# Two pairs of small matmuls put side by side in a fused transformer block, and two column loads put later

## The chip, the cores and the metric

The kernel runs on one core of one Trainium2 chip. A core has TensorE (PE, matrix products, accumulating in eight PSUM banks), VectorE (DVE), ScalarE (ACT), GpSimd (POOL) and SyncE (SP), which in this kernel does nothing but issue DMAs; sixteen DMA engines carry them out. The metric is the device time of one execution in microseconds. The times of the kernel before are 783.44, 783.46 and 783.54 us, median 783.46.

## The reference

One transformer block on 2048 tokens of width 1024: a linear attention with 32 heads, then a gated feed-forward network of width 3584, both modulated by a vector `c`.

```python
mod = (_silu(c) @ w_mod).reshape(c.shape[0], 6, 1, -1)
sa, ca, ga, sb, cb, gb = (mod[:, 0], ..., mod[:, 5])
h = _layernorm(x) * (1 + ca) + sa
x = x + ga * attention(h, wqkv, wo)
h = _layernorm(x) * (1 + cb) + sb
x = x + gb * (gelu(h @ w_gate) * (h @ w_up) @ w_down)
```

In the attention, `phi(t) = where(t > 0, t + 1, exp(t)) + 1e-06` is taken of the queries and keys, and

```python
kv  = einsum('bhsd,bhse->bhde', pk, v)
z   = einsum('bhsd->bhd', pk)
num = einsum('bhqd,bhde->bhqe', pq, kv)
den = einsum('bhqd,bhd->bhq', pq, z) + 1e-06
o   = num / den
```

Each of the six vectors of `mod` has 1024 values. `sa` and `ca` are the first shift and scale, `ga` the first gate, `sb` and `cb` the second shift and scale, `gb` the last gate.

## The kernel before

**Stages.** The first normalization, keys and queries fill the first 127 us. Then, up to about 192 us, comes the stage that the change edits: 24 tiles of `m_tile` (line 895), each 16 matmuls that sum over all tokens the product of keys and inputs; from these come, for each group of four heads, `kv_prod` (line 913, eight products with the value weights, masked by VectorE into `kvt`, line 917) and `w2_pair` (line 1196, `kvt` times the output weights, copied by ScalarE into `w`, line 1198). From about 192 us on `wo_mm` (line 1266) multiplies the scaled queries with `w`, 16 chunks of 128 tokens, each followed by VectorE's addition to `x` (x1, line 1274), the statistics and normalized rows of the second normalization on ScalarE and GpSimd, and a DMA transpose into `h2a` or `h2b` (line 703). At 242 us the first products of the feed-forward network begin (line 1440). They read transposed rows that have been modulated by the second scale and shift (`mod2`, line 724, on VectorE; `mod2_act`, line 753, on ScalarE), sums of them (`s_sum`, tile `ss`, line 1395) and sums of the gate and up weights (`t_sum`, tile `tp`, line 1415). The rest of the span is this network.

**The vectors of mod.** `sa` and `ca` are made at the start. `ga`, `sb`, `cb` and `gb` are made by VectorE in pieces of 512 columns: eight accumulations per piece (`macc`, lines 816 and 819, and 796 and 798 for `gb`), which leave on each partition a part of the sum, then a split into a high half (ScalarE, lines 825 and 803) and a low half (VectorE, lines 829 and 804; tiles `hl` and `hlg`), both bf16. `mod_rows` (line 840) sums these over the partitions with matmuls by a 128x32 matrix of ones: four pieces at a time, each to its own 32 partitions of one PSUM bank, first the four high, then the four low ones. `mod_store` copies the bank with ScalarE (line 847) and stores four partitions to DRAM (line 849). From there `ga` and `gb` are loaded as rows spread over the partitions (`row_load`, line 855), `sb` and `cb` as columns of 128 partitions x 8 (line 1213): elements of 4 bytes. `cb1` (line 1749) adds 1 to the scale on VectorE.

**den.** `den` (line 1223) multiplies a masked `z` (tile `z32`) of 128x32 with the queries, 64 matmuls for all tokens in two calls: `den0` for the first two token groups of 512, `den1` for the other two. A call has eight rounds of four matmuls to 32 partitions each. VectorE adds 1e-6 (line 1228) and takes the reciprocal (line 1229) into one tile `rdc`; SyncE stores it (line 1231), and `rb_load` (line 1243) loads it back, spread over 32 partitions at a time, four loads of 256 KB per half of a token group. `pq_scale` (line 1256) multiplies the queries by it.

**What sets the order.** TensorE's and SyncE's instructions run in the order in which the program writes them. `HOOK` (line 1284) says what is written behind which of the 24 tiles: `modp` is the rows of `sb` and `cb`, `gbr` those of `gb`. For VectorE, ScalarE and GpSimd a planner (`reorder`) sorts the instructions of the stage up to the chunks of `wo_mm` by due times, which it works back from who reads a result; what is written after that keeps the written order (`SLOT`, beside the chunks). Every DMA of SyncE is in one queue, on one of eight lanes in turn, and is issued only when the DMA eight places before it has landed. A bank, a tile or a lane that is used again waits for its last user by semaphores, which the program derives from what each instruction reads and writes.

Of the kernel before, what the change touches and what calls it, by code (L numbers as in the profile page):

```python
# [38 lines left out]
OFF_TMP = OFF_GUH + 4096  # L39
# [11 lines left out]
OFF_ROW = OFF_CONST + 4096  # L51
# [279 lines left out]
def bass_adaLN_cond__linear_attn_block__geglu_ffn__prompt_kernel(  # L331
# [18 lines left out]
    with ExitStack() as es:  # L350
# [6 lines left out]
        def at(name, shape, dty, off):  # L357
            return nc.alloc_sbuf_tensor_at(name, shape, dty, offset=ABASE + off, align_bytes=4)
# [46 lines left out]
        MROW = [at(f"mrow{i}", [P, 512], f32, OFF_ROW + i * 2048) for i in range(2)]  # L405
        MROW0 = at("mrowa", [P, 256], f32, XHO[2])
        WMG = [at(f"wmg{i}", [P, 4, 512], bf16, HBO[3] + i * 4096) for i in range(2)]
        MRG = at("mrg", [P, 256], f32, OFF_TMP + 4096)
        HLG = at("hlg", [P, 2, 2, 512], bf16, OFF_TMP)
# [35 lines left out]
        def r_sm(name):  # L445
            return [(SMO[name], SMO[name] + SMSZ[name], name)]

        def r_smc(name, c_, w):
            return [(SMO[name] + c_ * w, SMO[name] + (c_ + 1) * w, name)]

        def r_x(c_, c0=0, c1=D):
            return [(OFF_XALL + (c_ * HP + c0) * 2, OFF_XALL + (c_ * HP + c1) * 2, "xall")]
# [24 lines left out]
        def r_wv(g):  # L477
            return [(OFF_WK + g * 2048, OFF_WK + (g + 1) * 2048, "wv")]
# [4 lines left out]
        def r_pq(sg, k0=0, k1=NG, s0=0, s1=SGW):  # L483
            return r_t8(PQO[sg], f"pq{sg}", k0, k1, s0, s1)
# [19 lines left out]
        def r_w(off, name, dc, c0=0, c1=D):  # L504
            return [(off + (dc * D + c0) * 2, off + (dc * D + c1) * 2, name)]
# [25 lines left out]
        def r_rb(i, h, g0=0, g1=NG):  # L531
            return [(OFF_RB[i] + (h * NG + g0) * 1024, OFF_RB[i] + (h * NG + g1) * 1024, f"rb{i}")]

        def r_2k(off, name):
            return [(off, off + 2048, name)]
# [7 lines left out]
        def pr(b):  # L543
            return [(b * 2048, (b + 1) * 2048)]

        def PS(b, c0=0, c1=512):
            return ps_all[:, b * 512 + c0: b * 512 + c1]
# [18 lines left out]
        def pset_writer(b, o):  # L566
            for t_ in pr(b):
                sch.ps.set_writer(t_[0], t_[1], o)
# [94 lines left out]
        def ln_nmean(c_):  # L663
            gop(lambda e: e.tensor_scalar(MVA[:, c_, 0:1], STA[:, c_, 0:1], -1.0 / D, None, op0=ALU.mult), rd=r_smc("st", c_, 48), wr=r_smc("mv", c_, 8), note=f"nmean {c_}")
# [119 lines left out]
        def gb_load(j, q):  # L784
            sch.dma(Q, lambda e: e.dma_start(WMG[q][:], wm_v[:, 4 * q:4 * q + 4, (10 + j) * 512:(11 + j) * 512]), wr=r_wmg(q), note=f"wmg{j}.{q}")
# [3 lines left out]
        def r_hlg(j, h):  # L789
            return [(OFF_TMP + (2 * j + h) * 1024, OFF_TMP + (2 * j + h + 1) * 1024, "hlg")]  # L790
# [15 lines left out]
        o_gb = [None]  # L806

        def gb_rows():
            mod_rows(((0, 2, 5, lambda j, h: (HLG[:, j, h, :], r_hlg(j, h))),))
            o_gb[0] = mod_store(2, 5, MRG, [(OFF_TMP + 4096, OFF_TMP + 5120, "mrg")], 2)  # L810

        def mod_acc(k, dc):
            i, a = k % 2, k % 2
# [18 lines left out]
        def mod_rows(parts):  # L832
            for k0, n, bank, src in parts:
                o = None
                w = n * P
                for h in range(2):
                    for j in range(4):
                        ap, rng = src(k0 + j * n // 4, h)
                        ap = ap[:, j * w % 512:j * w % 512 + w]
                        o = sch.op(T, lambda e, h=h, j=j, ap=ap, bank=bank, w=w: e.matmul(  # L840
                            ps_all[32 * j:32 * (j + 1), bank * 512:bank * 512 + w], ONES[:, :], ap, start=(h == 0), stop=(h == 1)),
                            rd=rng + r_sm("ones"), pwr=(pr(bank) if h == j == 0 else ()), note=f"modr{k0}.{h}.{j}")
                pset_writer(bank, o)

        def mod_store(n, bank, dst, rng, row):
            w = n * P
            sch.op(A, lambda e: e.activation(dst[:, 0:w], ps_all[:, bank * 512:bank * 512 + w], ACTF.Copy),
                   prd=pr(bank), wr=rng, note=f"mrow{row}")
            return sch.dma(Q, lambda e: e.dma_start(scr_row[row, 0:n, :].rearrange("a (h b) -> (a h) b", b=w), dst[0:128:32, 0:w]), rd=rng, note=f"mrow{row}.st")
# [309 lines left out]
        for g in range(NG):  # L1159
            task(nk + g // 2, lambda g=g: sch.dma(Q, lambda e: e.dma_start(WV[:, g, :, :], wqkv_v[:, :, 2 * D + g * P:2 * D + (g + 1) * P]),  # L1160
                                                  wr=r_wv(g), note=f"wv{g}"))
# [45 lines left out]

        def mod_pass():
            assert mdone[0] >= 48 and not late
            mod_rows(((2, 4, 5, hl_src),))  # L1210
            o_r = mod_store(4, 5, MROW[1], r_2k(OFF_ROW + 2048, "mrow1"), 1)
            for dst, nt, a0 in ((SBT, "sbT", 0), (CBT, "cbT", 2)):
                sch.dma(Q, lambda e, dst=dst, a0=a0: e.dma_start(dst[:, :], scr_row[1, a0:a0 + 2, :].rearrange("a (b p) -> p (a b)", p=P)),
                        wr=r_sm(nt), deps=[o_r], note=nt)

        HW = SGW // 2

# [20 lines left out]
        def rb_load(sg, hs=(0, 1)):  # L1238
            i = sg % 2
            for h in hs:  # L1240
                made = []
                for k in range(HPG):
                    made.append(sch.dma(Q, lambda e, h=h, k=k: e.dma_start(
                        RB[i][32 * k:32 * (k + 1), h, :, :].rearrange("p a b -> p (a b)"),
                        scr_rd[sg, h, k:k + 1, :, :].rearrange("k g t -> k (g t)").to_broadcast([32, NG * HW])),
                        wr=r_rb(i, h) if k == 0 else (), deps=made[0].deps if k else [o_rd[sg // 2]], note=f"rb{sg}.{h}.{k}"))
                rb_ops[sg, h] = made
# [13 lines left out]
        def wo_mm(c_, b0, gs):  # L1261
            sg, ci = divmod(c_, CPG)
            last = [None, None]
            for g in gs:
                for half in range(2):
                    last[half] = sch.op(T, lambda e, g=g, half=half: e.matmul(  # L1266
                        PS(b0 + half), PQ[sg][:, g, ci * P:(ci + 1) * P], W2[:, g, half * 512:(half + 1) * 512],
                        start=(g == 0), stop=(g == NG - 1)),
                        rd=r_pq(sg, g, g + 1, ci * P, (ci + 1) * P) + r_w(OFF_WK, "w2", g, half * 512, (half + 1) * 512),
                        pwr=(pr(b0 + half) if g == 0 else ()), note=f"wo c{c_} g{g} h{half}")  # L1270
            if gs[-1] == NG - 1:
                for half in range(2):
                    pset_writer(b0 + half, last[half])
                x1_ops[c_] = sch.op(V, lambda e: e.scalar_tensor_tensor(XALL[:, c_, :], ps_all[:, b0 * 512:(b0 + 2) * 512], 1.0, XALL[:, c_, :],
                                                           op0=ALU.mult, op1=ALU.add, accum_out=STA[:, c_, 0:1]),
                       prd=pr(b0) + pr(b0 + 1), rd=r_x(c_), wr=r_x(c_) + r_smc("st", c_, 48),
                       deps=[s_ops[0, 0, 1]] if c_ == 13 else [], note=f"x1 c{c_}")
                if c_ < 2 * CPG:
                    ln_nmean(c_)
# [1 line left out]
        wo_load(0)  # L1281
        wo_load(1)
        tiles = [(g, k) for g in range(4) for k in range(3)] + [(g, 0) for g in range(4, NG)] + [(g, k) for g in range(4, NG) for k in (1, 2)]
        HOOK = {0: "ga", 6: "kv0", 8: "w0", 9: "kv1", 11: "w1", 12: "kv2", 14: "w2 modp", 15: "kv3 z32", 16: "den0", 17: "w3 rb0.0 rb0.1", 18: "",
                19: "kv4", 20: "w4 den1 ps0.0", 21: "gbr", 22: "ps0.1", 23: "rb2.0"}
        st = {}

        def hook_run(f):
            if f[:2] == "kv":
                kv_prod(int(f[2:]), 4)  # L1290
            elif f == "ga":
                ga_pass()
            elif f == "gbr":
                assert mdone[0] == 64
                gb_rows()
            elif f == "modp":
                mod_pass()
            elif f == "z32":
                z32()
            elif f[:3] == "den":  # L1300
                st[int(f[3:])] = den(int(f[3:]), 5)
                st[int(f[3:])]()
            elif f[:2] == "ps":
                pq_scale(int(f[2]), int(f[4]), GH[0] + GH[1])
            elif f[:2] == "rb":
                rb_load(int(f[2]), (int(f[4]),))
            elif f[0] == "w":
                w2_pair(int(f[1:]))

        for n, (g, k) in enumerate(tiles):  # L1310
# [13 lines left out]
            if n == 11:  # L1324
                gb_load(1, 0)
                gb_load(1, 1)
            for f in HOOK.get(n, "").split():
                hook_run(f)
# [8 lines left out]
        wo_mm(1, 2, E6[5:])  # L1337
        rb_load(1)
        rb_load(2, (1,))
        wo_mm(2, 4, E6[:4])  # L1340
        w2_pair(7)
        wo_mm(2, 4, E6[4:])
# [624 lines left out]
```

## Time and profile before

| | |
|---|---|
| median of 3 runs | 783.46 us |
| the profiled execution | 783.52 us |
| its span | 781.7 us |
| TensorE busy | 774.5 us, granted clock 1.0 |
| VectorE, ScalarE busy | 641.9 us, 376.3 us |
| `sbT` and `cbT`, issue to landing | 3.2 us, 3.1 us |
| rb loads, issue to landing, median | 6.9 us |

In a timeline a row is one instruction or a run of equal ones: its start in us from the span's start, its length, engine, line, operation, tile written and tiles read, shape, and in brackets how long the engine sat idle before it and what ended that. For matmuls `128*32` is the part of the array used. SPq is SyncE's DMA queue; its length is the time of issuing, not of the transfer. A stretch lists each engine's busy time and number of instructions, then the granted clock, the mean busy share of the sixteen DMA engines and what they moved.

### The profile page before, as it was taken

To read this page: it belongs to the slowest core of one execution; us is meant where nothing else is said; L and a number is where in the kernel's file an instruction comes from. 1 tells how busy PE (TensorE), PEld (TensorE's weight loads), DVE (VectorE), ACT (ScalarE), POOL (GpSimd) and SP (SyncE) were. 2 spreads that over 40 slices of the span, in tenths; PEclk is the share of its full clock that TensorE was granted. 3 is DMA by queue.
4 is the path that set the end of the run, shared out by engine and by line. 5 is a ranking of instruction groups with operands and counts; after the bars stand their busy time and mean duration, and the time that the engine had idled before them with its cause. 6 is when DMAs were issued, how large, how long until landed. Compare 5 with 4: busy or idle time off the path is not lost.

```text
span 781.7 us, 10762 instructions
## 1 busy us (share of the span) xinstructions
PE 774.5 (99%) x3867; PEld 497.4 (64%) x3867; DVE 641.9 (82%) x954; ACT 376.3 (48%) x631; POOL 47.0 (6%) x126
## 2 busy tenths in 40 slices
PE   8999999999999999999999999999999999999998
PEld 4444445666445667677676767677676576677766
DVE  6699988896689877787989888888989888676767
ACT  2497743243566487778655565555555211111111
POOL 2031300000331012100000000000000000000000
DMA  9879749939999247867353866435356334444331
GB/s 289 250 166 252 156 84 260 229 70 182 216 270 248 82 128 215 226 184 214 93 152 107 246 207 180 141 102 160 94 150 218 112 115 152 145 141 123 113 128 60
DMA packets 196844, 130.22 MB, mean 167 GB/s; under 512 B 69420, under 2 KB 182324, under 8 KB 195768
## 3 DMA queue, kind: packets, MB, share of 16 engines
q1 hardware_dynamic: 196776, 129.55, 61.0%
q8 instruction: 30, 0.49, 0.3%
q14 instruction: 22, 0.18, 0.1%
q10 hardware_dynamic: 16, 0.00, 0.0%
HBM read 92.55 MB, written 23.35 MB: 148 GB/s over the span
## 4 chain that ended last, share of the span: by engine, by line
PE 97%; SPq 1%; DMA 1%; DVE 0%; issue 0%; DVEq 0%
PE ps_all L1440 45%; PE ps_all L1654 21%; PE ps_all L895 7%; PE ps_all L1266 7%; PE ps_all L931 7%; PE ps_all L880 6%; PE ps_all L1575 1%; DMA wmq<-in_w_mod_dram 1%; SPq L598 1%; SPq L603 1%; PE ps_all L913 0%; PE ps_all L1196 0%; SPq L592 0%; PE ps_all L1223 0%; PE ps_all L766 0%; PE ps_all L840 0%
## 5 line engine op out<-in xcount | busy, mean ns | idle before, releaser
L1440 PE MATMUL ps_all<-ss,tp 128*128 128x512 f32 x896 | 214.3, 396 | 0.0
L1440 PEld LDWEIGHTS ps_all<-ss,tp 128*128 128x128 f32 x896 | 168.3, 188 | 37.7 <-DVE ss L1395 0.3
L1654 PE MATMUL ps_all<-dt,sb 128*128 128x512 f32 x424 | 102.5, 398 | 0.0
L1440 PE MATMUL ps_all<-h2a,wt 128*128 128x512 bf16 x448 | 101.6, 380 | 0.0
L1463 ACT ACTIVATE ge<-ps_all 128x512 f32<-128x512 f32 x112 | 64.1, 597 | 73.8 <-DVE ps_all L1451 62.0
L1654 PEld LDWEIGHTS ps_all<-dt,sb 128*128 128x128 f32 x424 | 79.6, 188 | 18.4 <-DVE sb L1630 0.3
L1458 DVE TENSOR_TENSOR ps_all<-ps_all,es 128x512 f32<-128x512 f32 x54 | 37.5, 699 | 49.7 <-ACT es L1448 49.3
L1470 DVE TENSOR_TENSOR ys<-ge,ps_all 128x512 bf16<-128x512 f32 x112 | 74.4, 684 | 3.4 <-PE ps_all L1654 0.5
L1440 PEld LDWEIGHTS ps_all<-h2a,wt 128*128 128x128 bf16 x448 | 37.9, 97 | 57.2 <-ACT ps_all L1445 16.9
L1415 DVE TENSOR_TENSOR tp<-wt 128x1024 fp32r<-128x1024 bf16 x56 | 68.1, 1216 | 2.1 <-DMA wt<-in_B_w_up_dram 2.1
L1415 DVE TENSOR_TENSOR tp<-wt,tp 128x1024 fp32r<-128x1024 bf16 x56 | 68.2, 1219 | 0.0
L880 PE MATMUL ps_all<-wk,h1T 128*128 128x512 bf16 x248 | 56.7, 379 | 0.3 <-DVE h1T L724 0.2
L931 PE MATMUL ps_all<-h1T,wq 128*128 128x512 bf16 x256 | 56.7, 379 | 0.0
L1266 PE MATMUL ps_all<-w,pq 128*128 128x512 bf16 x256 | 56.3, 379 | 0.0
L1440 PE MATMUL ps_all<-ar,tp 128*128 128x512 f32 x224 | 55.5, 390 | 0.0
L869 ACT ACTIVATE eb<-ps_all 128x512 f32<-128x512 f32 x64 | 36.3, 593 | 37.7 <-PE ps_all L880 15.3
L1654 PE MATMUL ps_all<-wd,ya 128*128 128x512 bf16 x212 | 48.5, 380 | 0.0
L1440 PEld LDWEIGHTS ps_all<-ar,tp 128*128 128x128 f32 x224 | 42.1, 188 | 8.8
L1445 ACT ACTIVATE ps_all<-ps_all 128x512 f32<-128x512 f32 x56 | 32.6, 582 | 27.1 <-PE ps_all L1440 27.1
L931 PEld LDWEIGHTS ps_all<-h1T,wq 128*128 128x128 bf16 x256 | 24.9, 98 | 30.0
L1266 PEld LDWEIGHTS ps_all<-w,pq 128*128 128x128 bf16 x256 | 24.7, 98 | 29.9 <-ACT w L1198 0.3
L1625 ACT ACTIVATE sb<-ya 128x896 fp32r<-128x896 bf16 (+1 forms) x16 | 14.5, 913 | 58.8 <-PE ps_all L1654 58.8
(140 smaller groups left out, 977.5 us busy)
## 6 DMA issues: line engine op xcount, KB each, us to landing
wt<-in_B_w_gate_dram SPq DMA_DIRECT2D x28, 512.0 KB, 4.1
wt<-in_B_w_up_dram SPq DMA_DIRECT2D x28, 512.0 KB, 5.3
scr_y<-ys SPq DMA_DIRECT2D x28, 512.0 KB, 3.2
ya<-scr_y SPq DMA_DIRECT2D x14, 896.0 KB, 5.9
rb<-scr_rd SPq DMA_DIRECT2D x32, 256.0 KB, 6.9
wd<-in_B_w_down_dram SPq DMA_DIRECT2D x7, 1024.0 KB, 7.9
wmst<-in_w_mod_dram SPq DMA_DIRECT2D x6, 1024.0 KB, 5.7
wmq<-in_w_mod_dram SPq DMA_DIRECT2D x8, 512.0 KB, 6.8
```

What stands on the lines that cost most here:

```text
L869: sch.op(A, lambda e: e.activation(EB[i][:, :], PS(bank), ACTF.Exp), prd=pr(bank), wr=rng, note=f"{note}.exp")
L880: o = sch.op(T, lambda e, dc=dc: e.matmul(PS(bank), H1[sg][:, ci, dc, :], W_[:, dc, jg * 512:(jg + 1) * 512], start=(dc == 0), stop=(dc == ...
L895: o = sch.op(T, lambda e, c_=c_: e.matmul(PS(bank, 0, n), PK[c_][:, g * P:(g + 1) * P], xrow(c_, o_, o_ + n), start=(c_ == 0), stop=(c_ == ...
L931: o = sch.op(T, lambda e, dc=dc: e.matmul(PS(b), WQ[:, dc, qc * P:(qc + 1) * P], H1[sg][:, :, dc, :], start=(dc == 0), stop=(dc == NDC - 1 ...
L1266: last[half] = sch.op(T, lambda e, g=g, half=half: e.matmul(PS(b0 + half), PQ[sg][:, g, ci * P:(ci + 1) * P], W2[:, g, half * 512:(half + ...
L1415: sch.op(V, lambda e: e.tensor_tensor(TP[k][:], in0, in1 if k in (0, 2) else in1[:], ALU.subtract), rd=r0 + r1, wr=r_tp(k), deps=[x1_ops[7 ...
L1440: o = sch.op(T, lambda e, l_=l_, r_=r_, dc=dc: e.matmul(PS(b), l_, r_, start=fresh and dc == 0, stop=dc == ND2 - 1, skip_group_check=True) ...
L1445: sch.op(A, lambda e: e.activation(PS(BB + t), PS(BA + t), ACTF.Copy), prd=pr(BA + t), pwr=pr(BB + t), note="pcp")
L1458: sch.op(V, lambda e: e.tensor_tensor(PS(BC + t), PS(BC + t), ES[t][:, :], ALU.add), prd=pr(BC + t), rd=r_2k(OFF_ES[t], f"es{t}"), pwr=pr( ...
L1463: sch.op(A, lambda e: e.activation(GE[i][:, :], PS(b), ACTF.Gelu_apprx_tanh), prd=pr(b), wr=r_2k(OFF_GE[i], f"ge{i}"), note="gelu")
L1470: sch.op(V, lambda e: e.tensor_tensor(YS[s_][:, 2 * h:2 * h + 2, t, :], q(GE[i][:, :]), q(PS(b + 1)), ALU.mult), rd=r_2k(OFF_GE[i], f"ge{i ...
L1654: o = sch.op(T, lambda e, l_=l_, r_=r_, j=j, dst=dst: e.matmul(dst, l_[:, 0, :], r_, start=(k in (1, 5) or own is not None) and j == js[0] ...
```

## The change

Four things are moved; no instruction is added or removed.

- The rows of `sb` and `cb` (`modp`) go from behind tile 14, where they follow `w2`, to behind tile 16, ahead of `den0`, and from bank 5 to bank 6.
- The rows of `gb` (`gbr`) go from behind tile 21 to behind tile 20, right after `den1`, and from bank 5 to bank 4. `den1` goes ahead of `w4`.
- The stores of both kinds of rows go with them.
- The two column loads of `sb` and `cb` are cut out of `mod_pass` into `mod_in`, which is called after the rb loads of the second token group and of half of the third, among the first chunks of `wo_mm`.

With the new places the planner also gives VectorE and ScalarE another order in this stage: `kvt` of the second to fourth group and the eighth `wofold` are earlier or later by one to three accumulations; the addition and the reciprocal of `den0` come ahead of the first product for the second half of `gb` and of the low half of its first half; `kvt` of the fifth group comes ahead of the last two accumulations; on ScalarE each copy of rows comes at its rows' new place. GpSimd's order is the same. On SyncE's queue the store of `gb`'s rows now stands ahead of a transpose that it followed.

```diff
         def gb_rows():
-            mod_rows(((0, 2, 5, lambda j, h: (HLG[:, j, h, :], r_hlg(j, h))),))
-            o_gb[0] = mod_store(2, 5, MRG, [(OFF_TMP + 4096, OFF_TMP + 5120, "mrg")], 2)
+            mod_rows(((0, 2, 4, lambda j, h: (HLG[:, j, h, :], r_hlg(j, h))),))
+            o_gb[0] = mod_store(2, 4, MRG, [(OFF_TMP + 4096, OFF_TMP + 5120, "mrg")], 2)
...
         def mod_pass():
             assert mdone[0] >= 48 and not late
-            mod_rows(((2, 4, 5, hl_src),))
-            o_r = mod_store(4, 5, MROW[1], r_2k(OFF_ROW + 2048, "mrow1"), 1)
+            mod_rows(((2, 4, 6, hl_src),))
+            o_sb[0] = mod_store(4, 6, MROW[1], r_2k(OFF_ROW + 2048, "mrow1"), 1)
+
+        o_sb = [None]
+
+        def mod_in():
             for dst, nt, a0 in ((SBT, "sbT", 0), (CBT, "cbT", 2)):
                 sch.dma(Q, lambda e, dst=dst, a0=a0: e.dma_start(dst[:, :], scr_row[1, a0:a0 + 2, :].rearrange("a (b p) -> p (a b)", p=P)),
-                        wr=r_sm(nt), deps=[o_r], note=nt)
+                        wr=r_sm(nt), deps=[o_sb[0]], note=nt)
...
-        HOOK = {0: "ga", 6: "kv0", 8: "w0", 9: "kv1", 11: "w1", 12: "kv2", 14: "w2 modp", 15: "kv3 z32", 16: "den0", 17: "w3 rb0.0 rb0.1", 18: "",
-                19: "kv4", 20: "w4 den1 ps0.0", 21: "gbr", 22: "ps0.1", 23: "rb2.0"}
+        HOOK = {0: "ga", 6: "kv0", 8: "w0", 9: "kv1", 11: "w1", 12: "kv2", 14: "w2", 15: "kv3 z32", 16: "modp den0", 17: "w3 rb0.0 rb0.1", 18: "",
+                19: "kv4", 20: "den1 gbr w4 ps0.0", 22: "ps0.1", 23: "rb2.0"}
...
         rb_load(1)
         rb_load(2, (1,))
+        mod_in()
         wo_mm(2, 4, E6[:4])
```

## The prediction

> **What bounds the kernel now.** First the page: which engine is full, and what the chain that ended last runs over. TensorE is busy for 99% of the span and the chain is 97% TensorE, so a change counts only where it lengthens or shortens TensorE's own row of work, or where it makes TensorE wait.
>
> ```profile
> PE 774.5 (99%) x3867; PEld 497.4 (64%) x3867; DVE 641.9 (82%) x954; ACT 376.3 (48%) x631; POOL 47.0 (6%) x126
> ```
>
> Second, TensorE's timeline around the moved instructions (start, length; the length runs over the next start, so the starts are what counts).
>
> ```profile
> 165.00 0.59 PE L1196 MATMUL ps_all<-wo,kvt 128*128 128x512 bf16 x2
> 165.52 0.62 PE L840 MATMUL ps_all<-hl,ones 128*32 128x512 bf16 x8
> 166.07 1.19 PE L895 MATMUL ps_all<-xrow,pk 128*128 128x341 bf16 x7
> ...
> 171.26 1.06 PE L1223 MATMUL ps_all<-pq,z 128*32 128x256 bf16 x32
> 172.25 1.19 PE L895 MATMUL ps_all<-xrow,pk 128*128 128x342 bf16 x7
> ```
> ```profile
> 182.43 0.59 PE L1196 MATMUL ps_all<-wo,kvt 128*128 128x512 bf16 x2
> 182.96 1.06 PE L1223 MATMUL ps_all<-pq,z 128*32 128x256 bf16 x32
> 183.95 1.19 PE L895 MATMUL ps_all<-xrow,pk 128*128 128x342 bf16 x7
> ...
> 186.38 0.40 PE L840 MATMUL ps_all<-hlg,ones 128*32 128x256 bf16 x8
> ```
>
> The reader is to see four separate islands of 32-column work (128*32) between full 128*128 work: rows at 165.52, den at 171.26 and 182.96, rows at 186.38. Third, SyncE's queue timeline: where the two column loads stand, and what is issued where they go to.
>
> ```profile
> 173.70 0.37 SPq L1213 DMA_DIRECT2D sbT<-scr_row  x1
> 174.12 0.58 SPq L1213 DMA_DIRECT2D cbT<-scr_row  x1
> ...
> 193.45 12.44 SPq L1243 DMA_DIRECT2D rb<-scr_rd  x16
> 210.76 1.24 SPq L703 DMA_TRANSPOSE h2a<-xl  x1
> ...
> 218.83 0.57 SPq L1353 DMA_DIRECT2D wt<-in_B_w_gate_dram  x1
> 219.45 0.57 SPq L1353 DMA_DIRECT2D wt<-in_B_w_up_dram  x1
> ```
>
> Fourth, busy times by stretch (PE, PEld, DVE, ACT, POOL, clock, DMA share, GB/s), the stretch of VectorE's long run first, then that in which the two column loads move their data, then the end of the rb loads.
>
> ```profile
> 225.40:252.90 27.50, 27.50 (x128) 13.46 (x125) 27.17 (x42) 17.20 (x28) 3.24 (x5) 1.00 1.06 263
> 174.80:176.40 1.60, 1.60 (x12) 1.05 (x11) 1.56 (x3) 1.47 (x2) 0.00 (x0) 1.00 0.73 5
> 206.00:213.00 7.00, 7.00 (x35) 3.12 (x33) 7.00 (x14) 4.46 (x7) 5.10 (x10) 1.00 1.02 219
> ```
>
> Fifth, VectorE's timeline, then TensorE's at the end of that run.
>
> ```profile
> 214.04 0.16 DVE L1749 TENSOR_SCALAR cb1T<-cbT 128x8 f32<-128x8 f32 x1
> ...
> 225.33 1.22 DVE L1415 TENSOR_TENSOR tp<-wt 128x1024 fp32r<-128x1024 bf16 x1 [2.11 <-DMA wt<-in_B_w_up_dram]
> ```
> ```profile
> 251.65 1.21 DVE L1395 TENSOR_TENSOR ss<-h2a,h2b 128x1024 fp32r<-128x1024 bf16 x1
> ```
> ```profile
> 252.92 2.12 PE L1440 MATMUL ps_all<-ss,tp 128*128 128x512 f32 x8
> ```
>
> This is what matters most. VectorE waits 2.11 us for the first up weights, starts at 225.33, is then busy 27.17 of 27.50 us, and ends its last sum ss at 252.86; the product that reads it starts at 252.92, back to back on TensorE. So from the landing of those weights to 252.92 there is a path with no slack that TensorE joins without a gap: each microsecond by which the weights land later is a microsecond of TensorE idle.
>
> **The change, part by part.**
>
> *Two pairs in place of four islands (gain).* Into an island: the second w2 matmul at 182.65 streams its 512 columns in 0.216 us (the step of that group), so 182.86 against den's start at 182.96: 0.09 us. Out of it: the last of den's eight rounds starts at 172.05 and streams 0.107 us, against 172.25: 0.10 us. At 165.43 to 165.52 and 165.97 to 166.07 it is the same. One island fewer is 0.19 us, two are 0.38 us. Bounds: 0.19 (if a change of bank or stationary inside the pair costs one entry again) and 0.66 (the queue's waits named "issue" before L840 and L1223, 1.7 us in 5, 0.33 each, if both that go were on the path). I take 0.38, since starts are what TensorE's time is made of. The matmuls themselves, 16 of the rows and 64 of den, stay the same.
>
> *Rows of the last gate one tile earlier (a possible wait).* They now follow den of the other groups at the end of tile 20. TensorE gets to their second half (the low parts) at 182.43 - 0.19 (the first island gone) + 0.09 + 0.89 + 0.11 = 183.33. VectorE must have made the low part by then; before, it ended at 181.63 for rows at 186.38. The planner also moves VectorE's order: the first den's addition and reciprocal come ahead of the last gate's first product and of its other half's low part, and the fifth kvt comes ahead of the last two accumulations. By rows: addition at 172.54, reciprocal 0.46 later (as at 184.41 and 184.87), 1.66 for it, 0.46 and 0.65, five accumulations at 0.77 (4.65 us for six), so 179.6; kvt waits for its products, which end at 180.27 - 0.19; with its 0.20 VectorE is free at 180.3, two accumulations 181.85, and from there 1.67 as before (179.96 to 181.63, ScalarE's copy between): 183.5. So TensorE waits 0.2 us; behind it stand w2 and tile 21. Bounds 0 and 0.6 (kvt 0.3 later, as the addition came 0.3 after den). What was at 186.38 leaves the other end of the same sum.
>
> *Other banks (nothing).* The rows go to banks 6 and 4. Bank 6 was read by the w2 copy that ended at 166.71, rows at 170.7; it is wanted again by w2 at 174.4, and ScalarE's copy of the rows (0.59 us) stands right behind the mb copy of 171.4. Bank 4: kvt ends at 180.3, wanted at 183.2; its next user is at 191.4. The 0.38 us copy stands ahead of the w2 copy now, whose reader comes after 191.8. All are covered by 2 us or more; without that cover they would cost their own 0.4 to 0.6 us.
>
> *SyncE's queue.* The store of the second rows and of the gate's rows are each issued about a transfer's place elsewhere: the first 2 us later, where nobody needs it before 206 us; the second ahead of one transpose, which waited for an mb copy until 187.15 anyway. Gone from 173.70 are the two column loads, with the wait of 2.7 us for the store in front of them; the reciprocal's store and the eight rb loads behind it come up to 1 us earlier, and VectorE's 0.77 us wait for rb at 189.73 may go. TensorE waits for none of that, so it gains nothing.
>
> *The column loads behind the rb loads (the price).* They are 4-byte elements, 2048 of them. At 174.80 they kept the queues busy for 0.73 of 1.60 us, 1.17 us of all sixteen, with next to nothing beside them. Their new place is behind sixteen loads of 256 KB, in a queue that is full (DMA share 1.02), and ahead of the transposes, the x rows and the first weights. Lanes (one load waits for the eighth before it) let them out at about 206.8 and 208.0; the last rb data move at 213.9. Behind them everything is full until the weights land: 9.0 us at a share of 1.14 from 216.0. So the weights land 1.17 us later, 225.14 to 226.3, and VectorE's run and TensorE at 252.92 with them. Bounds: 0, if they fall into the poor stretch at 214.5 to 216.0 (36 GB/s only), and 2.4, if a 4-byte packet costs beside other load what the semaphore writes there cost, 18 to 20 ns where the idle queue shows 9 (both from the trace's packets, 2048 over sixteen queues). SyncE's issue may add, since a transpose takes 1.24 us to issue into a short queue and 3.21 into a full one. I take 1.1, nearest to the row of the same transfer. A gain is excluded: the queue only gets more work at this place.
>
> *VectorE's wait for the shift columns (nothing, once).* cb1T at 214.04 will wait for cbT, which lands at about 216. Five x1, one scaling and eight modulations stand behind it, and all end 2.11 us before VectorE waits anyway, 3.2 with the later weights; TensorE wants x1's banks at 225 at the earliest. Without the later weights the 2 us would just fit.
>
> Sum, against the profiled execution's own 783.52 us (span 781.7, 1.8 around it; 0.06 over the median of the runs): - 0.38 + 0.2 + 1.1 = + 0.9, 784.4 us.
>
> **Rivals.**
>
> *A: the column loads fill the poor stretch.* For it: from 214.5 to 216.0 the queues moved 36 GB/s although transposes were issued. Against it: that stretch stands right behind the rb loads' landing and the transposes' packets are slow in it, so it may just move behind the columns. Time: 783.52 - 0.38 + 0.2 = 783.3.
>
> *B, slower: the columns hold up the queue for 2 us or more.* Place: SyncE's queue from 208 us, until cbT's 1024 elements fit behind sbT's; then the transpose of 210.76 is issued late, and each one after it. For it: transposes of 2.9 to 3.6 us in this stretch. Against it: two loads of weights of 1024 packets each were issued in 0.57 us. At 2.4 us: 785.7; it decides, that is leaves the measured bound, from 1.7 us on (783.52 - 0.38 + 0.2 + 1.7 = 785.0). The Trainium skill ("DMA: Bandwidth & Descriptors", section "Latency and other measured facts") gives an HBM access as 0.2 us on average and 2 us at high load; by an estimate from it the columns, read from HBM under load, would take 2 us and the sum would be 785.3. No row of before shows 4-byte reads under load.
>
> *C: the pair saves nothing.* A change of bank and stationary inside the 32-column work drains as leaving it does, and the low part comes 0.6 late: 783.52 + 0.6 + 1.1 = 785.2. Against it: den's own 32 matmuls change stationary each time and start in rounds of 0.11 us.
>
> **How the numbers follow.** About 0.2% (1.57 us) is what a measurement of this kernel tells from no change: 781.9 to 785.0. Forecast 0.55 (783.8 to 785.1), A 0.22 (783.0 to 783.7), B 0.18 (785.1 to 786.5), C 0.05. The range leaves out the ends of A and B: 783.1 to 786.0. Faster by over 0.2% needs 1.57 us where the islands' whole upper bound is 0.66: 0.02. Slower: B and a little of the forecast and C, 0.23. Same 0.75.
>
> **What would show it.** Two islands, not four, and 0.19 us less at each of two places; the queue's "issue" waits of L840 gone but for the first rows. A wait of TensorE for hlg of 0.1 to 0.5 us near 183. Column loads issued after the sixteenth rb load, cb1T idle about 2 us for cbT, the first up weights landing at 226 instead of 225.1, and an idle TensorE of about 1 us at 252.9, named by ss. The prediction is wrong if the weights land as before (A), if TensorE idles 2 us there (B), or if a wait turns up elsewhere, first of all at kv or wo behind transposes of mtb.

## The result

| | median | runs |
|---|---|---|
| before | 783.44 us (783.14 to 783.68) | 11 |
| after | 785.69 us (784.49 to 786.94) | 11 |

The ratio is 1.003, with a 95% interval from 1.0022 to 1.0038: the changed kernel is slower by 2.25 us, or 0.29%, which is more than the 0.2% that a measurement tells from no change. The forecast of 784.4 was too low by 1.3; the time lies inside the range of 783.1 to 786.0, but it is that of rival B, 785.7.

The profiled execution of the changed kernel took 786.94 us, with a span of 785.1, and is the longest of its eleven. It was 1.07 us late already at 60 us, where every engine still has the same order, and is as late just ahead of the moved rows (the `kv_prod` that starts at 159.91 us in the kernel before starts at 160.98). Its times below are to be read with that in mind.

### The profile page after: what moved, and what is told of

It reads as the page before. It is cut to its first block, busy times and chain, and to the rows that moved or that the text cites. A ratio compares the mean times of both kernels' runs of the same rounds, so it can differ in the third digit from the quotient of the medians.

```text
span 785.1 us, 10760 instructions
## 1 busy us (share of the span) xinstructions
PE 775.3 (99%) x3867; PEld 497.6 (63%) x3867; DVE 641.8 (82%) x954; ACT 376.4 (48%) x631; POOL 48.1 (6%) x126
## 4 chain that ended last, share of the span: by engine, by line
PE 85%; SPq 4%; DVE 4%; DMA 3%; issue 2%; ACT 1%; POOL 1%; DVEq 0%; ACTq 0%; POOLq 0%
PE ps_all L1445 44%; PE ps_all L1659 21%; PE ps_all L895 7%; PE ps_all L931 5%; PE ps_all L880 4%; SPq L598 2%; PE ps_all L1270 2%; DMA xall<-in_A_x_dram 1%; PE ps_all L1580 1%; SPq L703 1%; SPq L603 1%; DVE ss L1400 1%; DVE xall L1278 1%; DMA wt<-in_B_w_up_dram 1%; DVE pq L1260 1%
```

## The profile after

First the page's busy times: no engine does more work than before (TensorE 774.5 there).

```profile
PE 775.3 (99%) x3867; PEld 497.6 (63%) x3867; DVE 641.8 (82%) x954; ACT 376.4 (48%) x631; POOL 48.1 (6%) x126
```

TensorE's timeline around the moved matmuls (start, length):

```profile
171.68 0.61 PE L840 MATMUL ps_all<-hl,ones 128*32 128x512 bf16 x8
172.12 1.05 PE L1227 MATMUL ps_all<-pq,z 128*32 128x256 bf16 x32
173.10 1.19 PE L895 MATMUL ps_all<-xrow,pk 128*128 128x342 bf16 x7
...
183.37 1.06 PE L1227 MATMUL ps_all<-pq,z 128*32 128x256 bf16 x32
184.26 0.44 PE L840 MATMUL ps_all<-hlg,ones 128*32 128x256 bf16 x8
184.63 0.60 PE L1196 MATMUL ps_all<-wo,kvt 128*128 128x512 bf16 x2
```

Four islands of 32-column work have become two. What that saves is read from two rows that no edit touched, a `kv_prod` ahead of the islands and the second chunk of `wo_mm` behind them, first in the kernel before, then in the changed one:

```profile
159.91 0.61 PE L913 MATMUL ps_all<-mtb,wv 128*128 128x128 bf16 x8
...
194.85 2.32 PE L1266 MATMUL ps_all<-w,pq 128*128 128x512 bf16 x10
```
```profile
160.98 0.61 PE L913 MATMUL ps_all<-mtb,wv 128*128 128x128 bf16 x8
...
195.53 2.32 PE L1270 MATMUL ps_all<-w,pq 128*128 128x512 bf16 x10
```

The delay falls from 1.07 us to 0.68: the pairs save TensorE 0.39 us up to here. No bracket stands behind the rows of `hlg`, so TensorE idles there for nothing that the profile shows.

SyncE's queue timeline, where the column loads now stand:

```profile
207.18 0.39 SPq L1217 DMA_DIRECT2D sbT<-scr_row  x1
208.29 0.55 SPq L1217 DMA_DIRECT2D cbT<-scr_row  x1
211.44 5.91 SPq L703 DMA_TRANSPOSE h2a<-xl  x1
217.40 0.58 SPq L592 DMA_DIRECT2D xall<-in_A_x_dram  x1
218.08 4.34 SPq L703 DMA_TRANSPOSE h2a<-xl  x2
222.47 0.57 SPq L1358 DMA_DIRECT2D wt<-in_B_w_gate_dram  x1
223.10 0.57 SPq L1358 DMA_DIRECT2D wt<-in_B_w_up_dram  x1
```

The first transpose took 5.91 us to issue where it took 1.24 before. The two behind the x rows took less than before (4.34 against 5.75), and the up weights left at 223.10, against 219.45: 3.65 later, or 2.97 without the 0.68. Then VectorE's timeline:

```profile
218.00 0.17 DVE L1754 TENSOR_SCALAR cb1T<-cbT 128x8 f32<-128x8 f32 x1 [3.26 <-DMA cbT<-scr_row]
...
228.71 1.23 DVE L1420 TENSOR_TENSOR tp<-wt 128x1024 fp32r<-128x1024 bf16 x1 [1.68 <-DMA wt<-in_B_w_up_dram]
...
255.03 1.21 DVE L1400 TENSOR_TENSOR ss<-h2a,h2b 128x1024 fp32r<-128x1024 bf16 x1
```

and TensorE's where the feed-forward network starts:

```profile
244.00 3.61 PE L1445 MATMUL ps_all<-h2a,wt 128*128 128x512 bf16 x16 [0.81 <-DVE xall L1278]
248.15 2.11 PE L1445 MATMUL ps_all<-ss,tp 128*128 128x512 f32 x8 [0.54 <-DVE xall L1278]
250.42 2.14 PE L1445 MATMUL ps_all<-ss,tp 128*128 128x512 f32 x8 [0.16 <-DVE ss L1400]
...
256.30 1.90 PE L1445 MATMUL ps_all<-ss,tp 128*128 128x512 f32 x7 [0.27 <-DVE ss L1400]
```

These four idle times are the loss. Against the same instructions of the kernel before, the delay steps from 0.68 to 1.65 at 244.00, to about 2.5 at 248.15, to 2.87 around 250.42 and from 2.92 to 3.38 at 256.30, and stays there to the end of the span (3.39). That is 2.7 us. Of these, 0.39 only use up what the pairs had saved, and 2.3 are left, beside 2.25 between the medians. The bracketed idle adds up to only 1.78, while the starts say 2.7: at each break TensorE also loses the overlap of two matmuls, some 0.16 us (one of 512 columns is shown 0.38 long and the next starts 0.216 after it), which makes most of the difference.

The chain of waits shows in one view how the delay reaches TensorE (start, length, what; the changed kernel):

```profile
210.13 1.25 ACT xl L660
211.44 5.91 SPq L703
...
223.10 5.42 DMA wt<-in_B_w_up_dram
228.71 1.24 DVE tp L1420
...
255.12 1.14 DVE ss L1400
256.30 2.14 PE ps_all L1445 x8
```

In the kernel before the same stretch of the chain is nothing but TensorE:

```profile
201.07 41.44 PE ps_all L1266 x192
...
253.11 1.93 PE ps_all L1440 x8
```

## The experiments

After this the theory was: the pairs gain 0.39 us, and the late place of the two column loads costs 2.7, because their 2048 elements hold up SyncE's queue ahead of everything that the network waits for. Its rivals: the cost is VectorE's new wait for `cbT` (3.26 us, with all later VectorE work behind it); it is the bare transfer of the elements on the DMA engines, whoever issues them; it is the place, whatever stands there; or something else of the change, the earlier rows of the gate or the pairs themselves, takes part in it. The expectations add the gain and the loss; the runs side by side show below that the two do not add.

### The columns ahead of the first rb loads

The changed kernel, with the column loads issued behind tile 17, ahead of the first rb loads. Every instruction of TensorE, VectorE and ScalarE keeps its order.

```diff
-        HOOK = {... 17: "w3 rb0.0 rb0.1", 18: "",
+        HOOK = {... 17: "w3 cols rb0.0 rb0.1", 18: "",
...
+            elif f == "cols":
+                mod_in()
...
         rb_load(2, (1,))
-        mod_in()
```

> The changed kernel with the two column loads behind the transpose of the fifth group, ahead of the first eight rb loads; rows and den paired as changed, orders of TensorE, VectorE and ScalarE the same as in the changed kernel. All three theories (issue: the columns' 2048 elements fill SyncE's queue and hold up the transposes; transfer: their time on the DMA engines delays the weights; wait: VectorE's wait for the columns delays what is behind it) put the whole loss on the late place: 783.44 - 0.4 = 783.0 us, and the first transpose into h2a issued in about 1.2 us. If the pairing itself costs (late low part, other banks), 783.8 or more.

Measured: 783.11 us (782.6 to 783.39, 11 runs) against 783.31 (28 runs), ratio 0.9996 (0.9987 to 1.0005). SyncE's queue:

```profile
210.52 1.23 SPq L703 DMA_TRANSPOSE h2a<-xl  x1
...
219.24 0.57 SPq L1359 DMA_DIRECT2D wt<-in_B_w_up_dram  x1
```

The loss is gone with the place of the two loads alone, and so is the long transpose. Nothing else of the change has a cost that can be measured.

### The columns alone

The kernel before, with nothing moved in the program but the two loads, to the late place. The planner then also gives VectorE and ScalarE another order in places between 150 and 182 us; TensorE does not notice it (from the `kv_prod` to the second chunk of `wo_mm` it takes 34.94 us as before, 159.82 to 194.76).

```diff
-            o_r = mod_store(4, 5, MROW[1], ...)
+            o_sb[0] = mod_store(4, 5, MROW[1], ...)
...
+        def mod_in():
             for dst, nt, a0 in ((SBT, "sbT", 0), (CBT, "cbT", 2)):
...
         rb_load(2, (1,))
+        mod_in()
```

> The kernel before with nothing changed but the place of the two column loads (late, as in the changed kernel). If the place is the whole loss: 783.44 + 2.7 = 786.1 us, first transpose issued in 5 to 6 us. If pairing has a part in it: under 785.0.

Measured: 785.76 us (785.44 to 786.66, 5 runs) against 783.31, ratio 1.0033 (1.002 to 1.0045): 2.45 us. SyncE's queue:

```profile
210.68 4.56 SPq L703 DMA_TRANSPOSE h2a<-xl  x1
...
221.57 0.57 SPq L1358 DMA_DIRECT2D wt<-in_B_w_up_dram  x1
```

One part of the change makes the whole loss. The hold-up was a little shorter here than in the changed kernel's execution, 4.56 against 5.91 us; one trace of each does not show whether that lies in the kernel or in the execution.

### VectorE's wait, without the late loads

The columns back right behind the store of their rows, where the kernel before has them; `cb1T` is made to wait for the landing of the first transpose (`t2_ops[0]`) instead.

```diff
+            mod_in()
...
-        mod_in()
...
+            t2_ops[c_] = last_t[0]
...
-            sch.op(V, ... tensor_scalar(CB1T[:, :], CBT[:, :], 1.0, ...), rd=r_sm("cbT"), wr=r_sm("cb1T"))
+            sch.op(V, ... tensor_scalar(CB1T[:, :], CBT[:, :], 1.0, ...), rd=r_sm("cbT"), wr=r_sm("cb1T"), deps=[t2_ops[0]])
```

> The changed kernel with the column loads at their place of before, and cb1T on VectorE made to wait for the landing of the first transpose into h2a (about 217 us), so that VectorE waits about 3 us at the same place as in the changed kernel, with nothing late in the queue. Issue and transfer theory: the wait is covered by the later wait for the up weights, 783.0 to 783.3. Wait theory: 785 or more.

Measured: 783.37 us (782.37 to 783.94, 10 runs) against 783.31, ratio 0.9999 (0.999 to 1.0008). VectorE's largest wait from 200 to 260 us:

```profile
DVE cb1T L1757 <- DMA h2a<-xl: 2.9, 1, 2.9
```

The wait is there at nearly its full size (2.9 of 3.26 us) and costs nothing; it only takes the place of VectorE's later wait for the up weights, which is not among the waits of this kernel any more. The theory of VectorE's wait falls.

### The columns from ScalarE's queue

The changed kernel, with the column loads issued by ScalarE at about the same time, so that SyncE issues nothing between the last rb load and the first transpose.

```diff
-                sch.dma(Q, lambda e, dst=dst, a0=a0: e.dma_start(dst[:, :], scr_row[1, a0:a0 + 2, :]...
+                sch.dma(A, lambda e, dst=dst, a0=a0: e.dma_start(dst[:, :], scr_row[1, a0:a0 + 2, :]...
...
         rb_load(2, (1,))
-        mod_in()
...
         ln2_stats(1)
+        mod_in()
```

> The changed kernel with the two column loads issued at about the same time (207 us) by ScalarE, in ScalarE's own queue, so that they take the same DMA engines but no room in SyncE's queue. Issue theory: the first transpose is issued in about 1.2 us, and what is left is their transfer, 783.44 - 0.4 + 0 to 1.2 = 783.0 to 784.2. Transfer theory (all of the loss is DMA time): 785.7 as changed. Wait theory: cbT lands at about 210, before cb1T is due, so 783.0.

Measured: 783.93 us (783.5 to 784.93, 10 runs) against 783.31, ratio 1.0008 (0.9999 to 1.0017). ScalarE's and then SyncE's queue:

```profile
205.92 0.40 ACTq L1217 DMA_DIRECT2D sbT<-scr_row  x1
206.35 0.58 ACTq L1217 DMA_DIRECT2D cbT<-scr_row  x1
```
```profile
210.96 1.23 SPq L703 DMA_TRANSPOSE h2a<-xl  x1
212.24 0.73 SPq L592 DMA_DIRECT2D xall<-in_A_x_dram  x1
213.22 6.80 SPq L703 DMA_TRANSPOSE h2a<-xl  x2
...
220.71 0.57 SPq L1357 DMA_DIRECT2D wt<-in_B_w_up_dram  x1
```

The first transpose is back at 1.23 us, and the loss falls from 2.25 to 0.62 us, though the same 2048 elements move at the same moment. So the bare transfer is not the whole price. It may not be free either. The interval holds 1, but in the trace two transposes at the next place of SyncE's queue take 6.80 us instead of 5.75, and the up weights and VectorE's work on them come 0.6 to 0.7 us later than before (table below).

### One load late, the other early

The changed kernel, with `cbT` (1024 elements, `mod_in(1)`) at the late place and `sbT` (`mod_in(0)`) right behind the store.

```diff
             o_sb[0] = mod_store(4, 6, MROW[1], ...)
+            mod_in(0)
...
         rb_load(2, (1,))
-        mod_in()
+        mod_in(1)
```

> The changed kernel, but only the load of cbT (1024 elements of 4 B) stays at the late place behind the 16 rb loads; the load of sbT goes back to right behind the store. Place theory (any load that stands there and waits for the rb data holds SyncE's queue): the full loss stays, about 785.7 us, with SyncE's first h2a transpose at 4 us or more. Elements theory, the hold-up in proportion to the elements: half of the 2.7 us less the 0.39 us of the islands, 783.3 + 1.35 - 0.39 = 784.3 us, the first transpose at about 3 us. Room theory (the queue holds one such load besides the rb loads, not two): only the transfer of 1024 elements is left, 783.3 + 0.5 - 0.39 = 783.4 us, the first transpose at 1.2 us as in the kernel before.

Measured: 784.4 us (783.6 to 785.36, 10 runs) against 783.26 (27 runs), ratio 1.0013 (1.0004 to 1.0023): 1.14 us. SyncE's queue, then VectorE's first work on the up weights:

```profile
210.50 3.91 SPq L703 DMA_TRANSPOSE h2a<-xl  x1
...
220.86 0.57 SPq L1359 DMA_DIRECT2D wt<-in_B_w_up_dram  x1
```
```profile
226.41 1.23 DVE L1421 TENSOR_TENSOR tp<-wt 128x1024 fp32r<-128x1024 bf16 x1 [1.61 <-DMA wt<-in_B_w_up_dram]
```

Half of the elements, about half of the loss: 1.14 us (0.3 to 1.8 by the interval) of 2.25. One such load holds up the transpose too (3.91 us), so the theory of room for one falls, and the place alone does not cost the whole.

### The same bytes in 256 runs

The changed kernel, both loads at the late place, 4 KB each as before, but read as 128 runs of 32 B. The values of the second shift and scale then stand in another order, so the second norm is modulated with values of other features; everything else is computed as in the reference.

```diff
-                ... scr_row[1, a0:a0 + 2, :].rearrange("a (b p) -> p (a b)", p=P)
+                ... scr_row[1, a0:a0 + 2, :].rearrange("a (p b) -> (a p) b", b=8)
```

> The changed kernel, with both column loads at the same late place and of the same 4 KB each, but read in runs of 8 neighbouring values: 128 elements of 32 B for each load in place of 1024 of 4 B. The second shift and scale then stand in another order over partitions and columns, so the second norm's modulation is computed with values that belong to other features; all else is the same. Place or wait theory: nothing changes, about 785.7 us, the first h2a transpose again at over 4 us. Elements theory (their number fills the queue and the engines, not the place or the bytes): 783.0 to 783.2 us, the first transpose at 1.2 us, the weights' issue back within 0.5 us of the kernel before.

Measured: 783.09 us (782.38 to 783.92, 10 runs) against 783.26, ratio 0.9996 (0.9987 to 1.0005). SyncE's queue, then VectorE:

```profile
205.54 0.34 SPq L1217 DMA_DIRECT2D sbT<-scr_row  x1
206.76 0.34 SPq L1217 DMA_DIRECT2D cbT<-scr_row  x1
209.61 1.24 SPq L703 DMA_TRANSPOSE h2a<-xl  x1
...
218.44 0.57 SPq L1358 DMA_DIRECT2D wt<-in_B_w_up_dram  x1
```
```profile
215.62 0.17 DVE L1754 TENSOR_SCALAR cb1T<-cbT 128x8 f32<-128x8 f32 x1 [2.69 <-DMA cbT<-scr_row]
```

Same place, same bytes, nearly the same wait of VectorE (2.69 us), and no loss: the elements make it. The theory of the place falls. This run changes the number and the size of the elements together; that the number counts at one size is what the run with one load late shows.

### The columns right behind their store

The changed kernel with the loads where the kernel before has them.

```diff
             o_sb[0] = mod_store(4, 6, MROW[1], ...)
+            mod_in()
...
         rb_load(2, (1,))
-        mod_in()
```

> The changed kernel, with the column loads right behind the store of their rows, where the kernel before has them; the pairing of rows and den stays. If the late place is the whole of the loss, what is left is the gain of two islands less: 783.3 - 0.39 = 782.9 us, 782.7 to 783.3. If the earlier last gate or the pairing itself costs time elsewhere (in the place of the other tiles' work), 783.5 us or more.

Measured: 783.13 us (782.65 to 783.99, 11 runs) against 783.26, ratio 0.9999 (0.999 to 1.0007). The first transpose takes 1.23 us to issue, and the up weights leave at 218.72. As with the early columns, nothing of the loss is left. The four kernels that keep the pairs and lose nothing (early columns, VectorE's wait, runs of 32 B, behind the store) have medians from 0.20 us below to 0.06 us above the kernel before, and each interval holds 1: a version that beats both kernels has not been shown.

Even without the late loads the gain of the pairs does not come out whole. In this trace TensorE has saved 0.33 us at the second chunk of `wo_mm` (34.61 us from the `kv_prod` at 159.23, against 34.94). Then VectorE's last sum and the product that reads it:

```profile
250.87 1.21 DVE L1400 TENSOR_TENSOR ss<-h2a,h2b 128x1024 fp32r<-128x1024 bf16 x1
```
```profile
252.14 2.11 PE L1445 MATMUL ps_all<-ss,tp 128*128 128x512 f32 x8
```

The product starts 0.06 us after the sum's end, as in the kernel before (252.86 and 252.92). From the `kv_prod` on it is only 0.10 us earlier than there, as much as VectorE's first work on the up weights is.

### The runs side by side

Each row is one profiled execution, with times from the start of the `kv_prod` named above (159.91 us in the kernel before), so that what happened ahead of the stage drops out. "Transpose" is the time to issue the first one into `h2a`, "up issued" and `tp` the issue of the first up weights and VectorE's first work on them. The next three columns are differences from the kernel before: `tp`, TensorE at the second chunk of `wo_mm`, and the time of this execution from the `kv_prod` on. The last is the difference of the medians.

| kernel | elements late | transpose | up issued | `tp` starts | `tp` | TensorE | execution | median |
|---|---|---|---|---|---|---|---|---|
| before | 0 | 1.24 | 59.54 | 65.42 | 0 | 0 | 0 | 0 |
| columns alone | 2048, SyncE | 4.56 | 61.75 | 67.47 | +2.05 | 0.00 | +2.01 | +2.45 |
| changed kernel | 2048, SyncE | 5.91 | 62.12 | 67.73 | +2.31 | -0.39 | +2.35 | +2.25 |
| one load late | 1024, SyncE | 3.91 | 60.78 | 66.33 | +0.91 | -0.44 | +0.88 | +1.14 |
| ScalarE's queue | 2048, ScalarE | 1.23 | 60.22 | 65.99 | +0.57 | -0.39 | +0.54 | +0.62 |
| runs of 32 B | 256 of 32 B | 1.24 | 59.29 | 65.17 | -0.25 | -0.39 | -0.31 | -0.17 |
| behind the store | 0 | 1.23 | 59.49 | 65.32 | -0.10 | -0.33 | -0.13 | -0.13 |
| early columns | 0 | 1.23 | 59.27 | 65.18 | -0.24 | -0.31 | -0.29 | -0.20 |
| VectorE's wait | 0 | 1.23 | 59.15 | 64.79 | -0.63 | -0.31 | -0.31 | +0.06 |

In every row the execution's time follows the later of the two, `tp` or TensorE, within 0.06 us, and nothing else has to be called in. A sum of the two does not fit: for the changed kernel it would be +1.92, for one load late +0.47. TensorE's 0.39 us and the weights' delay lie on two paths that meet at the product that reads `ss`; the later one sets the time, and what the other has saved is spent waiting there.

## Why the prediction was right or wrong

**In short.** The measured 785.69 lies inside the stated range, but that is luck for the forecast's own mechanism: it had 783.8 to 785.1 for itself, and the time is that of rival B, to which it gave 0.18. Two steps of its sum failed, the price of the column loads and the adding up.

**Two pairs for four islands: right, as far as TensorE's own row goes.** -0.38 was taken, -0.39 measured in the changed kernel. The other kernels with the pairs show -0.31 to -0.44 over the same stretch, and the columns alone show 0.00. So rival C, in which the pair saves nothing, is excluded by the traces.

**The gate's rows one tile earlier: the mechanism was right, the size small.** VectorE's low part ended at 184.35, with TensorE at the rows' first half from 184.26 and the second half next, so the low part was nearly late, as worked out; but no idle time is shown there. The 0.2 taken belongs near 0; what little there is sits in the -0.39.

**Other banks, the early part of SyncE's queue, VectorE's wait for `cbT`: right, they cost nothing.** The last of these was the one that looked dangerous, 3.26 us of VectorE idle, and the run that keeps 2.9 us of it, with the columns back behind their store, shows that it is covered.

**Zero slack from the landing of the up weights to TensorE: right, and this carries the case.** But the idle time did not come as one gap of about 1 us at 252.9 named by `ss`. It came in four, and the first two, at 244.00 and 248.15, are named by `xall`: VectorE's chunk additions, which free PSUM banks, stand in VectorE's written order behind the late `tp`, so they were late before `ss` was.

**The adding up: a step that failed.** The sum took - 0.38 + 0.2 of TensorE's row and 1.1 of the weights' landing together. By the prediction's own reading TensorE joins a path without slack at 252.92, so what TensorE gains ahead of that point cannot be taken off a delay of that path. Its own terms give 783.52 + 1.1 = 784.6 for the forecast, 785.9 for rival B at 2.4, and no gain, 783.5, for rival A. The table shows it: in the changed kernel `tp` came 2.31 us later and the execution took 2.35 longer, with all of TensorE's 0.39 spent waiting.

**The column loads behind the rb loads: a step that failed.** It took the elements' transfer, 1.1 us, and left out what it mentioned in half a sentence, that SyncE's issue may add. The term measured 2.45 alone (medians) and 2.3 in the changed kernel. Its upper bound of 2.4 rested on 4-byte packets getting dearer beside other load, and that is not what happened: between 214 and 216 us they took 9 to 10 ns each, as in the idle queue of the kernel before. What happened is rival B's mechanism at rival B's place, with a size of 2.3 where 2.4 was put: SyncE did not get through the issue of the first transpose until 217.35, after the last elements had moved (at about 216.0), and so did not feed the x rows, the other transposes and the weights. Two stretches of 8 us from the end of the rb loads show it, first the kernel before, then the changed one (the last two numbers are the mean busy share of the DMA engines and GB/s):

```profile
213.50:221.50 8.00, 8.00 (x39) 3.63 (x38) 7.13 (x18) 5.62 (x9) 3.56 (x11) 1.00 1.13 231
```
```profile
214.20:222.20 8.00, 8.00 (x39) 3.63 (x38) 4.74 (x10) 4.07 (x6) 3.24 (x9) 1.00 0.84 145
```

The DMA engines were less busy than before, not more: they were short of work, because the issue was held. Rival A, in which the columns fill the poor stretch, had the place right (they ran right behind the rb data), but the weights landed later all the same.

Rival B's estimate from the Trainium skill ("DMA: Bandwidth & Descriptors", section "Latency and other measured facts": an HBM access 0.2 us on average, 2 us at high load) gave 785.3, near the result for another reason. The runs of 32 B read the same DRAM under the same load and cost nothing, so a slow access alone is not the price. The evidence against rival B was that weights of 1024 packets each were issued in 0.57 us; those rows say nothing of 1024 elements that wait behind 16 rb loads.

**What stays open.** How much of the 2.3 us is the elements' own time and how much the held issue cannot be told apart cleanly: from ScalarE's queue some 0.5 us was left, but there, too, it shows as a longer issue of SyncE's next transposes. What it is inside the issue that runs out of room, and at how many elements, was not measured; 1024 are too many behind these loads, 256 of 32 B are not.

## What to carry to other kernels

Count a small DMA's elements, not its bytes, before it is put behind a long queue: 8 KB in 2048 elements held up the next issue by 3 to 5 us and cost 2.3 to 2.5 us at the end, while 8 KB in 256 runs cost nothing at the same place. When a load moves, look at what the same issuing engine sends next and at how much slack the receiver of that has; here it was zero, and the receiver of the moved load itself had plenty. A saving on the bounding engine does not come off such a delay: where two paths meet without slack, take the later of the two and not their sum.

## What the hardware showed that was not expected

- A DMA's issue can be held by elements of earlier DMAs: the same transpose took 1.24, 3.91 and 4.56 to 5.91 us to issue with 0, 1024 and 2048 small elements ahead of it in a busy queue.
- Loads issued by ScalarE did not get past SyncE's. They were issued at 205.92 and 206.35, and up to 212 us, while the rb data moved, no packet of theirs ran; these are the packets by queue in the run with ScalarE's queue (q1 is SyncE's, q10 ScalarE's), from 206 to 212 us and then from 212 to 217:

```profile
q1 hardware_dynamic: 232, 1.25, 98.2%
```
```profile
q1 hardware_dynamic: 606, 0.53, 107.0%
q10 hardware_dynamic: 2080, 0.01, 25.4%
```

The Trainium skill ("DMA: Bandwidth & Descriptors", section "Queues, rings and completion order") has each DMA engine take turns between the queues that have work, a packet at a time. No such turns are seen here between these two queues up to 212 us: the elements landed 10.2 us after their issue, nearly all of them behind the rb data that had been issued earlier. Whether they waited in the DMA engines or had not been handed to them was not measured, so this run does not decide against that rule.
